# Batch 3's tails are cast and turned earlier, batch 5's loads move to GpSimd's queue (sliding-window attention, then a GELU block)

## Chip, cores and metric

The kernel runs on one core of a Trainium2 chip. The metric is device time in microseconds, as the median of several runs; a profile of one further execution comes with it. Engines are named as in the profile: PE is TensorE (PEld its weight loads), DVE is VectorE, ACT is ScalarE, POOL is GpSimd and SP is SyncE, whose queue of DMA issues is SPq.

## The reference

```python
# q, k, v: (8 batches, 8 heads, 576 positions, 64), fp32
scores = (q @ k.T) / 8                        # per batch and head
mask = |pos_i - pos_j| <= 32                  # others get -1e9
attn = softmax(scores);  x = attn @ v         # -> x: (4608 tokens, 512)
h = x @ w_in                                  # (512, 2048)
g = 0.5 * h * (1 + tanh(sqrt(2/pi) * (h + 0.044715 * h**3)))
out = g @ w_out                               # (2048, 512), fp32
```

## The kernel before

The 4608 tokens are nine tiles of 512. Tile `t` of the second part (`w_in`, Gelu, `w_out`) runs while the attention of batch `b = t + 1` is worked on between its matmuls, so a batch is always one tile ahead. The order of all instructions on every engine is written out by hand (the pools run in manual schedule); waits between engines follow from the tiles that instructions read and write.

A tile has two stretches. In the first, `ffn_in` makes 16 blocks of 128 hidden columns, four matmuls of 128x512 each (L594), and ScalarE takes the Gelu of each (L602). Its loop over `fc` carries extra steps of the attention at given `fc`. In tiles 3 and up this stretch is written as a list of steps (`MIX_1`, run by `in_mixed`), in which step `keys` of tile 3 turns batch 4's keys and issues batch 5's loads, and step `tails` turns batch 4's tails. In the second stretch, a loop over `i` from 0 to 111 issues one matmul of the product with `w_out` each (L794; seven products of 16 matmuls instead of eight), and a plan (`PLAN_1` for tile 1, `PLAN_2` for tile 2, `PLAN` after) says at which `i` a score (`s`), a mask (`m`), a weighing (`v`) or a spread (`x`) of the next batch comes. Scores `s0` and `s1` stand at `i == 7`, `s2` at 35, `s3` and the score of the tails, `s4`, at 63; `b0` and `b1`, casts of the next batch's keys, at 63 too.

The attention needs queries and keys transposed. Positions 0 to 511 and the last 64 (the tails) go separate ways:

- Batches 1 to 3 have their tails of queries and keys in one tile `tr`. `cast_tails` (L358) casts it to fp16 as `t`, `trans_tails` transposes it on TensorE (L363), and ScalarE copies the result to `KL` and `QT` (L365, L367).
- From batch 4 on, tails are cast by VectorE (L419 for queries, L446 for keys) and transposed by DMA on SyncE's queue: `turn_queries` (L422) writes `QT`, `turn_key_tails` (L447) writes `KL`.
- The other positions are cast by VectorE (`turn_query` L427, `turn_keys` L437) and transposed by DMA on SyncE's queue (L431 to `QT`, L439 to `KT`, two pairs of heads at a time).

`load_qk(b)` issues the loads of a batch's queries (L208, 1 MB in one transfer) and keys (L200, four transfers of 256 KB); `load_tails` those of the tails (L214, L215 from batch 4 on). SyncE's queue works in the order of the program. GpSimd's queue carries the loads of the values, cast to fp16 on the way (`load_v` L223, `load_vt` L227), and the stores of the output (`store`, L754 and L756). Ahead of each batch's `load_v` GpSimd copies one column of `KL` to a tile `after` (L1039), which makes the load wait for that `KL`. In tile 1 GpSimd also casts batch 3's values (L1043).

The output tile `y` is stored in eight transfers a tile: four for the part C21 when it is done (L826, at `i == 95`), four at the tile's end in `ffn_last` (after L835).

Of the kernel before, what the change touches and what calls it, by code (L numbers as in the profile page):

```python
# [84 lines left out]
def kernel(  # L85
# [9 lines left out]
    nc = tc.nc  # L95
# [87 lines left out]

        return qk, tails, vs

    def load_qk(b):


        if b == 3:
            qr = raws[3]  # L190
        else:
            qr = rawp.tile([128, H, 256], FP32, name="qr", tag="q0")
            load_q(b, qr)
        kr = rawp.tile([128, 4, H, 64], FP32, name="kr", tag="k1" if b == 3 else "k0")
        if b > 3:
            raws[b] = [qr, kr]
        else:
            raws[b] = [qr, kr, tailp.tile([128, H, 64], FP32, name="tr", tag="tr"), None]
        for c in range(4):
            nc.sync.dma_start(kr[:, c, :, :],  # L200
                              k[b, :, 128 * c:128 * c + 128, :].rearrange("h p d -> p h d"))
        if b < 5:
            load_tails(b, nc.sync)
        if b == 3:
            load_vr(3)

    def load_q(b, qr):
        nc.sync.dma_start(qr, q[b, :, 0:512, :].rearrange("h (p j) d -> p h (j d)", j=4))  # L208

    def load_tails(b, queue):  # L210
        if b > 3:
            raws[b] += [tailp.tile([16, H, 256], FP32, name="qt", tag="vt"),
                        tailp.tile([64, H, 64], FP32, name="kt", tag="tr")]
            queue.dma_start(raws[b][2], q[b, :, 512:576, :].rearrange("h (p j) d -> p h (j d)", j=4))  # L214
            queue.dma_start(raws[b][3], k[b, :, 512:576, :].rearrange("h p d -> p h d"))  # L215
        else:
            queue.dma_start(raws[b][2][0:64, :, :], q[b, :, 512:576, :].rearrange("h s d -> s h d"))
            queue.dma_start(raws[b][2][64:128, :, :], k[b, :, 512:576, :].rearrange("h s d -> s h d"))
# [136 lines left out]
    def cast_tails(b, copy, half=slice(0, 128)):  # L355
        if len(halfs[b]) < 3:
            halfs[b].append(hp.tile([128, H, 64], FP16, name="t16", tag="t16"))
        copy(halfs[b][2][half, :, :], raws[b][2][half, :, :])  # L358
# [50 lines left out]
    def load_vr(b):  # L409
        vr = vrs[b] = rawp.tile([128, 4, H, 64], FP32, name="vr", tag="q1")  # L410
        for c in range(4):
            nc.sync.dma_start(vr[:, c, :, :],
                              v[b, :, 128 * c:128 * c + 128, :].rearrange("h p d -> p h d"))
# [36 lines left out]
    def open_and_turn(b):  # L450
        cast_open(b)
        for pr in range(NPAIR):
            turn_query(b, pr)
# [117 lines left out]
    def column(t, n):  # L571

        return n // 2 + 8 * (n % 2) if t else n
# [79 lines left out]
    def in_mixed(t):  # L653
        if "B" not in mixed:
            mixed["B"] = rawp.tile([128, 3, 512], FP32, name="sb", tag="q1")
        if t == NT - 2:
            mixed["A"] = rawp.tile([128, 3, 512], FP32, name="sa", tag="k0")

        place = {"00": (0, "b"), "01": (1, "c"), "11": (2, "c")}
        for step in MIX if t >= NT - 2 else MIX_1:  # L660
            kind, rest = step[0], step[1:]
            if step == "pair":
                pair_v(t + 1, nc.vector.tensor_copy)
            elif step == "load":
                if 3 < t < B - 2:
                    load_qk(t + 2)
            elif step == "keys":
                if t == 3:
                    turn_keys(4)
                    load_qk(5)  # L670
            elif step == ("f0" if t > 3 else "tails"):
                turn_queries(t + 1)
                if t == 3:
                    turn_key_tails(4)
                    load_tails(5, nc.sync)
            elif step == "f1":
                if t > 3:
                    turn_key_tails(t + 1)
                    if t + 2 < B:
                        load_tails(t + 2, nc.sync)  # L680
            elif step in ("f0", "tails"):
                pass
            elif kind in UNITS:
                in_product(kind, int(rest), t < NT - 2)
            elif kind == "s":
                n, unit = int(rest[0]), rest[1]
                (nc.scalar.copy if n == 1 or rest == "3B" else nc.vector.tensor_copy)(
                    mixed[unit][:, (0, 1, None, 2)[n], :], phs[unit, "a"])
            elif kind == "c":
                x, which = place[rest[1:]]  # L690
                x = mixed[rest[0]][:, x, :]
                nc.vector.tensor_tensor(x, phs[rest[0], which], x, op=ALU.add)
            elif kind == "g" and rest[0] in UNITS:
                r, c, j = int(rest[1]), int(rest[2]), UNITS[rest[0]]
                src = phs[rest[0], "a"] if rest[1:] == "10" else mixed[rest[0]][:, place[rest[1:]][0], :]
                nc.scalar.activation(gTs[t][:, 8 * r + 2 * j:8 * r + 2 * j + 2, 256 * c:256 * c + 256],
                                     src.rearrange("p (h c) -> p h c", h=2), AF.Gelu_apprx_tanh)
            elif kind == "g":
                fc = column(t, int(rest))
                nc.scalar.activation(gTs[t][:, fc, :], phs[fc], AF.Gelu_apprx_tanh)  # L700
            elif kind in PARTS:
                sums(t, int(rest), PARTS[kind])
            else:
                ffn_in(t, int(step), then=False)
# [271 lines left out]
    for t in range(NT):  # L976
        b = t + 1
        att = b < B
        if t:
            for fc in range(begun):  # L980
                ffn_in(t, fc, 3, 4, then=False)
            for fc in range(begun):
                gelu(t, fc)
            if b == 2:
                open_and_turn(2)
                combine(2, nc.vector)
                combine(3, nc.vector)
            elif att:
                if t >= LONE:
                    in_x(t)  # L990
                if b == 3:
                    turn_keys(b)
            if t >= NT - 2:
                if t == NT - 2:
                    in_x(t)
                in_mixed(t)
            elif t >= LONE:
                in_mixed(t)
            for fc in range(begun, NF if t < LONE else 0):
                ffn_in(t, fc)  # L1000
                if t == 1 and fc == 3:
                    turn_keys(2)
                    load_vr(2)
                    raws[2] = [None, None, raws[2][2], vrs[2], tailp.tile([64, H, 64], FP32, name="vt", tag="vt")]
                    nc.sync.dma_start(raws[2][4], v[2, :, 512:S, :].rearrange("h p d -> p h d"))
                    raws[3] = rawp.tile([128, H, 256], FP32, name="qr", tag="q0")
                    load_q(3, raws[3])
                    combine(4, nc.vector)
                if t == 1 and 6 <= fc < 10:
                    cast_v(2, fc - 6)  # L1010
                if t == 1 and fc == 6:
                    trans_tails(1, psO.tile([128, 8, 128], FP16, name="pt", tag="O"))
                if t == 1 and fc == 8:
                    cast_tails(2, nc.scalar.copy)
                if t == 1 and fc == 13:
                    trans_tails(2, psO.tile([128, 8, 128], FP16, name="pt", tag="O"), copy=nc.scalar.copy,
                                copy_q=nc.scalar.copy)
                if t == 2 and fc == 8:
                    cast_tails(3, nc.gpsimd.tensor_copy)
                if t == 2 and fc == 13:  # L1020
                    trans_tails(3, psO.tile([128, 8, 128], FP16, name="pt", tag="O"), copy=nc.scalar.copy,
                                copy_q=nc.scalar.copy)
                if t == 2 and fc == 8:
                    pair_v(b, nc.vector.tensor_copy)
                if t == LONE - 1 and fc in (8, 9, 10, 11):
                    in_w(nc.vector, "B", (8, 9, 10, 11).index(fc) + 1)
# [7 lines left out]
        if t in (1, 2):  # L1034
            load_qk(b + 1)
        ods = {}
        for i in range(113 if t else 65):
# [5 lines left out]
                    nc.gpsimd.tensor_copy(Vs[1][:, c, :, :], vrs[3][:, c, :, :])  # L1043
            if t == 1 and i == 98:
                open_and_turn(3)
            for act in plan.get(i, "").split():
                kind, at = act[0], int(act[act.index("@") + 1:]) if "@" in act else None
                g = int(act[1:].split("@")[0])
# [52 lines left out]
                elif kind == "v":  # L1101
                    bb, gg = group(g)
                    o, d = weigh(bb, gg, at)
# [59 lines left out]
```

## Time and profile before

| | |
|---|---|
| median of 3 runs | 296.35 us (295.05 to 297.62) |
| profiled execution | 296.1 us, span 294.2 us |
| TensorE's granted clock, mean | 0.992 |
| tile 2's Gelu stretch | about 86 to 100 us |
| tile 3's Gelu stretch, then its `w_out` stretch | about 117 to 131 us, 131 to 148 us |

A stretch's times are read from the windows of the profile. In a timeline, a line gives start and duration in us, the engine, the line of the kernel, the operation, output and inputs, and how many instructions of a kind were merged; square brackets hold the idle time of the engine before it and what ended it. For the queue of SyncE a line's duration is the time that the issue took, not the transfer; a transfer lands later.

### The profile page before, as it was taken

To read this page: it belongs to the slowest core of one execution; us is meant where nothing else is said; L and a number is where in the kernel's file an instruction comes from. 1 tells how busy PE (TensorE), PEld (TensorE's weight loads), DVE (VectorE), ACT (ScalarE), POOL (GpSimd) and SP (SyncE) were. 2 spreads that over 40 slices of the span, in tenths; PEclk is the share of its full clock that TensorE was granted. 3 is DMA by queue.
4 is the path that set the end of the run, shared out by engine and by line. 5 is a ranking of instruction groups with operands and counts; after the bars stand their busy time and mean duration, and the time that the engine had idled before them with its cause. 6 is when DMAs were issued, how large, how long until landed. Compare 5 with 4: busy or idle time off the path is not lost.

```text
span 294.2 us, 7438 instructions
## 1 busy us (share of the span) xinstructions
PE 285.1 (97%) x2993; PEld 197.4 (67%) x2993; DVE 227.5 (77%) x499; ACT 197.0 (67%) x323; POOL 87.7 (30%) x143
## 2 busy tenths in 40 slices
PE   8889999999999999999999999999999999999993
PEld 3535544557875588668766886688667877887783
DVE  4565369898987977998878798889888877875672
ACT  4875767879477776587558955895579667905800
POOL 3434325102228821400662236015600060016000
PEclk9979999999999999999999999999999999999998
DMA  7999998999999999999999799999930022005013
GB/s 217 265 332 411 353 305 223 254 183 197 253 224 190 234 223 184 215 216 168 140 176 269 163 144 208 234 124 115 192 83 2 3 73 72 0 3 144 0 47 98
DMA packets 114392, 51.02 MB, mean 173 GB/s; under 512 B 98471, under 2 KB 110247, under 8 KB 114102
## 3 DMA queue, kind: packets, MB, share of 16 engines
q1 hardware_dynamic: 89460, 38.67, 58.9%
q0 software_dynamic: 23776, 10.83, 23.3%
q10 hardware_dynamic: 1122, 1.06, 1.1%
q8 instruction: 23, 0.38, 0.6%
q14 instruction: 11, 0.09, 0.1%
HBM read 36.70 MB, written 9.44 MB: 157 GB/s over the span
## 4 chain that ended last, share of the span: by engine, by line
PE 81%; DMA 7%; SPq 5%; POOL 3%; issue 1%; DVE 1%; ACT 0%; ACTq 0%; POOLq 0%
PE mm L794 28%; PE ph L594 16%; PE mm L594 13%; PE pu L650 7%; DMA vr<-in_v_dram 4%; PE ps_s L485 3%; PE py L766 3%; PE mm L766 2%; SPq L200 2%; PE ps_d L512 2%; PE ps_o L522 2%; DMA qr<-in_q_dram 2%; DMA KL<-kt 2%; PE mm L650 1%; POOL out_dram L756 1%; PE ps_od L512 1%
## 5 line engine op out<-in xcount | busy, mean ns | idle before, releaser
L594 PEld LDWEIGHTS <-w_in 128*128 128x128 f16 x448 | 50.2, 113 | 38.7
L594 PE MATMUL ph<-xT,w_in 128*128 128x512 f16 x240 | 60.2, 379 | 0.0
L594 PE MATMUL mm<-xT,w_in 128*128 128x512 f16 x208 | 53.7, 379 | 0.0
L794 PEld LDWEIGHTS <-s 128*128 128x128 f16 x512 | 49.4, 98 | 6.1
L756 POOL DMA_DIRECT2D out_dram<-y x55 | 30.4, 561 | 72.1 <-DVE y L826 63.0
L794 PE MATMUL mm<-t,s 128*128 128x256 f16 x376 | 44.9, 273 | 0.0
L794 PEld LDWEIGHTS <-gT 128*128 128x128 f16 x384 | 36.1, 98 | 6.6 <-issue 0.2
L498 ACT ACTIVATE pe<-ps_s 128x960 f16<-128x960 f32 (+1 forms) x31 | 29.6, 976 | 14.0 <-PE ps_s L485 13.8
L602 ACT ACTIVATE gT<-mm 128x512 f16<-128x512 f32 x28 | 16.5, 599 | 24.8 <-PE mm L594 24.5
L794 PE MATMUL mm<-w_out,gT 128*128 128x256 f16 x256 | 32.6, 273 | 0.0
L737 DVE TENSOR_TENSOR s<-gT 128x512 f16<-128x512 f16 x64 | 27.3, 432 | 6.4 <-ACT gT L602 3.0
L602 ACT ACTIVATE gT<-ph 128x512 f16<-128x512 f32 x38 | 20.9, 606 | 7.0 <-PE ph L594 7.0
L110 ACT ACT_TABLE_LOAD x18 | 23.1, 1283 | 2.2 <-issue 1.9
L547 ACT ACTIVATE lt<-ps_d 128x480 f32<-128x480 f32 (+2 forms) x28 | 15.5, 555 | 12.6 <-PE ps_d L512 7.7
L548 ACT ACTIVATE lt<-lt 128x480 f32<-128x480 f32 (+3 forms) x36 | 21.1, 586 | 1.1
L507 DVE TENSOR_TENSOR pe<-pe,band 128x960 f16<-128x960 f16 x28 | 17.7, 651 | 2.7 <-ACT pe L498 2.6
L522 PEld LDWEIGHTS <-V 128*64 128x64 f16 x520 | 14.2, 113 | 6.2 <-DVE V L233 1.6
L700 ACT ACTIVATE gT<-ph 128x512 f16<-128x512 f32 x22 | 13.2, 601 | 4.8 <-PE ph L594 4.7
L794 PE MATMUL mm<-t,gT 128*128 128x256 f16 x128 | 16.2, 273 | 0.0
L557 DVE TENSOR_TENSOR xT<-ps_o,lt 128x480 f16<-128x480 f32 (+5 forms) x26 | 13.4, 533 | 3.2 <-PE ps_o L522 2.8
L1039 POOL COPY after<-KL 128x1 f16<-128x1 f16 x4 | 1.2, 312 | 45.8 <-DMA KL<-kt 44.9
L223 POOL DMA_DIRECT2D V<-in_v_dram x16 | 14.3, 909 | 1.1 <-PE ps_o L522 0.4
(154 smaller groups left out, 488.5 us busy)
## 6 DMA issues: line engine op xcount, KB each, us to landing
kr<-in_k_dram SPq DMA_DIRECT2D x31, 256.0 KB, 6.3
qr<-in_q_dram SPq DMA_DIRECT2D x6, 1024.0 KB, 8.2
wst<-in_moe_w_in_dram SPq DMA_DIRECT2D x8, 512.0 KB, 6.6
vr<-in_v_dram SPq DMA_DIRECT2D x12, 256.0 KB, 6.0
wst<-in_moe_w_out_dram SPq DMA_DIRECT2D x2, 1024.0 KB, 11.6
wst<-in_moe_w_out_dram SPq DMA_DIRECT2D x4, 512.0 KB, 7.2
V<-in_v_dram POOLq DMA_DIRECT2D x16, 128.0 KB, 5.2
qr<-in_q_dram SPq DMA_DIRECT2D x7, 256.0 KB, 8.2
```

Of the source, the lines that this page charges most:

```text
L110: nc.scalar.add_instruction(mybir.InstLoadActFuncSet(name=nc.get_next_instruction_name(), act_func_set_id=which, ins=[], outs=[]))
L498: nc.scalar.activation(pe, ps[:, :, 0:w], AF.Exp, scale=SCALE)
L507: nc.vector.tensor_tensor(pe, pe, m.rearrange("k (o j) p -> k o j p", o=1).broadcast_to(list(pe.shape)), op=ALU.mult)
L522: nc.tensor.matmul(o[64 * h:64 * h + 64, cols].rearrange("d (j p) -> d j p", j=4)[:, :, p0 - q0:p1 - q0], Vs[b % 2][:, slot, 2 * pr + h, : ...
L547: nc.scalar.activation(lt[:, 0:n], d[:, 0:n], AF.Ln)
L548: nc.scalar.activation(lt[:, 0:n], lt[:, 0:n], AF.Exp, scale=-1.0)
L594: nc.tensor.matmul(ph, w_cols[:, dc, fc // 4, fc % 4, :], xT[:, dc, t * 512 % RING:t * 512 % RING + 512], start=(dc == 0), stop=(dc == 3))
L602: nc.scalar.activation(gTs[t][:, fc, :], phs[fc], AF.Gelu_apprx_tanh)
L650: nc.tensor.matmul(ps[:, 256 * h:256 * h + 256], lhs[:, d, h, :], rhs[:, d, :], start=(n in (0, 2, 4) and h == d == 0), stop=(h == d == 1) ...
L737: nc.vector.tensor_tensor(dst, x, y, op=op)
L756: eng.dma_start(out_v[b, j, q0 + p:q0 + p + e, cols], yo[m:m + e, cols])
L794: nc.tensor.matmul(pys["apart"][:, 0:256] if apart else py[:, blk, :], lhsT, wino[w][:, f, :], start=(new and i % (8 if one else 16) == 0) ...
```

## The change

Two moves. The cast of batch 3's tails (`cast_tails(3)`, on GpSimd in both versions) goes from block 8 of tile 2 to `i == 98` of tile 1, in the program's order behind the stores of C21 and ahead of the four of `ffn_last`; their transposes on TensorE, with ScalarE's two copies, go from behind block 13 of tile 2 to behind block 10. And `load_qk` takes a queue: batch 5's queries and keys, five transfers, are issued by GpSimd in place of SyncE, at the same step `keys` of tile 3. Its tails stay on SyncE's queue.

```diff
-    def load_qk(b):
+    def load_qk(b, queue=nc.sync):
...
-            load_q(b, qr)
+            load_q(b, qr, queue)
...
-            nc.sync.dma_start(kr[:, c, :, :],
+            queue.dma_start(kr[:, c, :, :],
...
-    def load_q(b, qr):
-        nc.sync.dma_start(qr, q[b, :, 0:512, :].rearrange("h (p j) d -> p h (j d)", j=4))
+    def load_q(b, qr, queue=nc.sync):
+        queue.dma_start(qr, q[b, :, 0:512, :].rearrange("h (p j) d -> p h (j d)", j=4))
...
                 if t == 3:
                     turn_keys(4)
-                    load_qk(5)
+                    load_qk(5, nc.gpsimd)
...
-                if t == 2 and fc == 8:
-                    cast_tails(3, nc.gpsimd.tensor_copy)
-                if t == 2 and fc == 13:
+                if t == 2 and fc == 10:
                     trans_tails(3, psO.tile([128, 8, 128], FP16, name="pt", tag="O"), copy=nc.scalar.copy,
                                 copy_q=nc.scalar.copy)
...
             if t == 1 and i == 98:
                 open_and_turn(3)
+                cast_tails(3, nc.gpsimd.tensor_copy)
```

## The prediction

> **What bounds the kernel now.** I read the page's first part, then the chain of work that ended last, then the list of waits of TensorE in the part of the span that the change touches, and then the timelines of the engines that it moves work between. The page says that TensorE is the wall:
>
> ```profile
> PE 285.1 (97%) x2993; PEld 197.4 (67%) x2993; DVE 227.5 (77%) x499; ACT 197.0 (67%) x323; POOL 87.7 (30%) x143
> ...
> PE 81%; DMA 7%; SPq 5%; POOL 3%; issue 1%; DVE 1%; ACT 0%; ACTq 0%; POOLq 0%
> ```
>
> No other engine is near 97%, so a gain can only come out of TensorE's idle time. The waits of TensorE from 86 us to the end of the span (who waited for whom, us in total, times, longest) are two:
>
> ```profile
> PE ps_s L485 <- DMA KL<-kt: 0.7, 1, 0.7
> PE pt L363 <- POOL t L358: 0.4, 1, 0.4
> ```
>
> The timelines show both. First the tails of batch 3 in tile 2 (start, duration, and in brackets the idle time before):
>
> ```profile
> 92.89 2.14 POOL L756 DMA_DIRECT2D out_dram<-y  x4
> 95.01 0.76 POOL L754 DMA_DIRECT2D out_dram<-y  x1
> 95.77 1.66 POOL L756 DMA_DIRECT2D out_dram<-y  x3
> 97.43 0.85 POOL L358 CAST t<-tr 128x512 f16<-128x512 f32 x1
> ...
> 98.33 0.40 PE L363 MATMUL pt<-idn,t 128*128 128x128 f16 x4 [0.45 <-POOL t L358]
> ```
>
> GpSimd issues tile 1's eight stores, then casts; TensorE waits 0.45 us for the cast. Second, the keys' tail of batch 4 in tile 3, as SyncE's queue and TensorE show it:
>
> ```profile
> 127.36 0.57 SPq L208 DMA_DIRECT2D qr<-in_q_dram  x1
> 128.03 6.30 SPq L200 DMA_DIRECT2D kr<-in_k_dram  x4
> 134.43 1.92 SPq L422 DMA_TRANSPOSE QT<-qt  x1
> 136.44 2.25 SPq L447 DMA_TRANSPOSE KL<-kt  x1
> ...
> 140.99 0.23 PE L485 MATMUL ps_s<-QT,KL 64*64 64x96 f16 x2 [0.72 <-DMA KL<-kt]
> ```
>
> The transpose that writes KL is issued behind batch 5's five loads and lands at 140.95; TensorE stood ready at 140.27. After that TensorE has no wait left to the end, so what is taken away at these two places reaches the end whole, and 0.45 + 0.72 = 1.17 us is all that there is to win.
>
> **The change, part by part.** *Cast and turn of batch 3's tails.* The moved instruction is one cast (0.85 us). In the changed program's order GpSimd runs it after the four C21 stores (92.89 to 95.01) and ahead of the other four, not ahead of all eight. Those four cannot be earlier either: the chain of work leads into them from L1043's casts, which wait for batch 3's values, landed at 90.53. So the cast runs at about 95.01 to 95.86, 2.42 us earlier than now. But TensorE asks for it earlier too. Without its stall it reaches the transposes at 98.33 - 0.45 = 97.88; a block of four matmuls is 0.865 us (96.86 to 94.27 is three blocks), so behind block 10 it reaches them at 97.88 - 2.59 = 95.29. The cast's end and the 0.05 us that TensorE needs after it give 95.91, so it waits 0.62 us in place of 0.45: **0.17 us lost**. Bounds: the chain shows 0.34 us of "issue" before 95.01, so a cast might start at 94.67; GpSimd's casts of this case took 0.60 (L347, 64 partitions) to 0.96 us (L1043). That gives a wait of 0.03 to 0.77 us, or -0.42 to +0.32. I take the row of the same cast, 0.85. Its cover: the two ScalarE copies behind the transposes (0.37 and 0.38 us) come between Gelus that wait 0.27 us for TensorE, thus three Gelus absorb them as now. The four stores that the cast passes go out 0.85 us later, about 104.95 instead of 104.10 for the last landing; VectorE writes their buffer again at 105.68 (L807), so 0.7 us of cover remains. The values' loads (L223) start 0.9 us earlier, since GpSimd ends with a store at 98.28 and the copy "after" no longer waits for ScalarE's KL; they land before batch 4's last keys (119.09) in either case. Both at nothing.
>
> *Batch 5's loads on GpSimd's queue.* SyncE loses five issues (127.36 to 134.33). Its next step, L422, waits for VectorE's four L419 casts, which end at 130.35, so it goes out near 130.4 instead of 134.43, four microseconds earlier; with the same 1.92 and 2.25 us of issue, L447 ends near 134.7 and lands, with the 2.26 us that it took here from the end of its issue, at 137.0. TensorE wants it at 140.27 (+0.17): a margin of 3.4 us, **0.72 us won**. Bounds: 0 to 0.72. GpSimd gains five issues. The nearest row is its own values' load with as many rows:
>
> ```profile
> 141.62 3.57 POOL L223 DMA_DIRECT2D V<-in_v_dram  x4
> ```
>
> 0.89 us each, 4.5 us in all, in a stretch in which it is idle (121.25 to 141.07). They wait there for earlier transfers of the same lane (lanes are used in turn, eight of them): the first for the store of 116.32, which landed at 120.64, the fourth and fifth for stores that landed at 124.58 and 127.11. So the queries' load goes out near 121.3 and the last keys near 127.2 to 128.1, where SyncE's last was out at 134.33. Behind them on GpSimd stand only the copy "after", which waits for KL (earlier now), the values' loads and the stores of 147: nothing is late by that. The total of bytes is the same.
>
> What the trace does not show is fp32 loads from GpSimd's queue beside SyncE's transposes. These share the 16 DMA engines. Batch 4's transposes for the queries and keys are issued at 117.60, 121.62 and 126.04 and land at 128.19, 128.50 and 129.71, with the stores of GpSimd's queue beside them until 128.2. The stores stand ahead of the new loads in that queue, so little changes before 127. The nearest row with loads in GpSimd's queue is batch 5's keys: issued at 144.57 and 146.33 beside the V loads they landed 8.0 and 10.6 us later. With these the first keys would land at 129.6 (needed at 131.2) and the second at 136.7 (needed by s2 at 135.4, late by 1.3 us). Best case 129.71 as now, worst 136.7: cost 0 to 1.3 us. I take 0, since the loads stand behind the stores and batch 4's transposes are mostly done when they begin; batch 5's met the V loads from their start.
>
> The loads must land for VectorE's key casts at 141.01 (now 139.34 for the last). From 128.1 as the last issue with the L200's longest landing of 12.8 us it would be 140.9: just in time. VectorE could be held until 142.8 before its mask L507 (142.77, read by TensorE at 145.22, 0.65 us long) is late, so I cost it at nothing.
>
> The Trainium skill, "SBUF — State Buffer", section on the two separate sides, under "A bandwidth-pool intuition that's wrong (but worth ruling out)", says that GpSimd cannot write a transfer's descriptors while VectorE holds their shared port, and gives about 3.1 us for a transfer that takes 0.62 alone. The 0.89 us above was measured beside VectorE's casts L427 and L437, so the trace does not show that here. By the page's figure the five would take 15.5 us, an estimate, and end near 137.
>
> **Sum.** +0.17 - 0.72 = -0.55 us. The profiled execution took 296.1 us with a span of 294.2, so it would take 295.55. The median of the runs is 296.35, 0.25 above the profiled one; on that scale the forecast is 295.8 us.
>
> **Rivals.** *The tails' wait goes as well* (cast starts at 94.67 and is short): -0.42 - 0.72 = -1.14, 295.2 us. For it, the 0.34 us of "issue"; against it, 0.85 for this very cast.
>
> *KL is as late as now*: its transpose shares the engines with loads that are still moving. For it, L422 in tile 4 needed 6.6 us from issue to landing with GpSimd's stores beside it; against it, 3.4 us of margin. Then +0.17, 296.5 us.
>
> *Slower: batch 4's keys are turned late because GpSimd's loads mix with the transposes.* Place: score s2 at 135.4 us, and before it s0 at 131.2. It decides from a landing later than 135.4 + 0.55. By batch 5's row it is 1.3 us; with KL then in time anyway, 1.3 + 0.17 - 0.72 = +0.75, 297.1 us; if the first pair is late by as much again as its margin (1.6 us), it is +2.4, 298.7. For it, batch 5's 8.0 and 10.6 us, and the 4.3 us that the first key transpose needed only to be issued here; against it, the stores ahead of the loads in the queue.
>
> *GpSimd's issues are held up by a busy VectorE*: if each took 3.6 us, what now four take together, the five would end near 139.3 and the last keys land 6.3 us later (L200's median), at 145.6; VectorE, in order, would hold its mask 2.8 us past the slack of 142.8: +2.25 us, 298.6. Against it, 0.89 us beside a busy VectorE. This is the rule of the Trainium skill's SBUF page above; the trace so far speaks against it.
>
> **How the numbers follow.** Forecast 0.47; tails' wait gone 0.10; KL as late as now 0.17; keys turned late 0.18; issues held up 0.08. All but the dear ends of the last two lie within 1% (2.96 us, about what a measurement of this kernel can tell from no change, its three runs spreading from 295.05 to 297.62). A gain over 1% would need more than all of TensorE's waits here: 0.03, for noise. Slower by over 1%: half of the last two, 0.13. Within: 0.84. The range goes from 294.8 (the best case less 0.4 for noise) to 298.4, just short of the dear ends; the forecast's own is 294.9 to 296.7.
>
> **What would show it.** Right: TensorE's wait before L363 about 0.6 us, behind block 10; GpSimd's cast between its fourth and fifth store; L422 issued near 130.4 and KL landed before 138; no wait of TensorE for KL, KT or QT in tile 3; span near 293.65. Wrong: a wait of TensorE at s0 or s2 of tile 3 on a KT transpose; the new loads taking over 1.5 us each on GpSimd; VectorE waiting at L437 for kr; or a wait before L363 under 0.2 us.

## The result and the profile after

The changed kernel takes 305.72 us (median of 6 runs, 304.97 to 308.07) against 296.06 us for the kernel before on the same chip; the ratio is 1.0353 (95% interval 1.0298 to 1.0408). In this document a ratio leaves out runs more than 1.5% above the fastest of their kernel, a median has them in. The profiled execution took 305.65 us with a span of 303.8 us, 9.6 us more than before. The page's first part and chain of the kernel after, to be read beside those of before:

```profile
PE 285.3 (94%) x2993; PEld 198.1 (65%) x2993; DVE 227.2 (75%) x499; ACT 196.8 (65%) x323; POOL 91.7 (30%) x148
...
PE 69%; DMA 14%; SPq 6%; DVE 5%; POOL 2%; issue 2%; ACT 1%; ACTq 0%; DVEq 0%; POOLq 0%
```

TensorE does the same work (285.3 us) but now has idle time, and transfers stand for twice the share of the chain. The waits of TensorE from 80 us on are these two (us in total, times, longest):

```profile
PE ps_s L485 <- DMA KT<-k: 9.6, 1, 9.6
PE mm L794 <- DVE y L817: 0.2, 1, 0.2
```

Neither of the two waits of before is left: not the one at L363 and not the one for KL. In their place stands one of 9.6 us for KT, the keys of batch 4, at the first scores of tile 3, which the prediction had named as a sign that it is wrong. The chain of the kernel after around that place (start, duration):

```profile
119.48 0.86 PE mm L594 x4
120.34 0.15 PE pu L650 x2
120.49 19.02 DMA KT<-k
139.51 0.04 issue
139.55 1.01 PE ps_s L485 x24
```

The transpose that writes KT's first pair is issued at 120.49 us and lands 19.02 us later; in the kernel before it took 6.9 us (121.62 to 128.50). The timelines of GpSimd and of SyncE's queue in the kernel after show what stands beside it:

```profile
120.19 0.93 POOL L208 DMA_DIRECT2D qr<-in_q_dram  x1 [0.33 <-DMA out_dram<-y]
121.12 1.78 POOL L200 DMA_DIRECT2D kr<-in_k_dram  x2
124.93 1.76 POOL L200 DMA_DIRECT2D kr<-in_k_dram  x2 [2.03 <-DMA out_dram<-y]
...
116.07 4.32 SPq L431 DMA_TRANSPOSE QT<-q  x1
120.49 10.23 SPq L439 DMA_TRANSPOSE KT<-k  x2
130.81 2.24 SPq L422 DMA_TRANSPOSE QT<-qt  x1
133.14 1.19 SPq L447 DMA_TRANSPOSE KL<-kt  x1
```

GpSimd issues the five loads without trouble, 0.9 us each. SyncE's two key transposes need 10.23 us to be issued, 5.69 before. L422 goes out at 130.81, right behind them, and lands only at 142.40; KL lands at 143.01. The transposes of the tails are thus late too, as those of the keys are.

The wait costs more than its length. In the windows of the kernel after (us, busy us of each engine with its count, then TensorE's granted clock, DMA share and GB/s) the clock falls while TensorE stands:

```profile
130.00:134.00 4.00, 0.00 (x0) 0.00 (x0) 2.20 (x7) 1.08 (x1) 0.00 (x0) 1.00 1.29 133
134.00:144.30 10.30, 4.75 (x57) 3.51 (x58) 0.88 (x2) 2.74 (x4) 0.84 (x2) 0.50 1.15 92
144.30:148.00 3.70, 3.70 (x71) 2.99 (x70) 2.71 (x5) 1.64 (x3) 3.57 (x5) 1.00 1.22 79
```

TensorE stops at 129.91 and goes on at 139.55, so for about 4.7 us after the wait the clock is at a half. From s0 to the score of the tails TensorE needs 150.60 - 139.55 = 11.05 us; before it was 140.99 - 131.22 - 0.72 of waiting = 9.05. So 2.0 us are lost to the clock. "TensorE: Matmul & The Clock Gate" of the Trainium skill, under "What's actually happening", says that the clock halves after an idle stretch of some 3.4 us and comes back after as much work. Here it halved about 4.1 us after TensorE stopped and came back 4.7 us after it went on; but in run e1 below a wait of 2.45 us, which ended at 96.18, was already followed by 3.4 us at half:

```profile
97.30:100.70 3.40, 3.40 (x10) 1.19 (x9) 2.12 (x5) 1.19 (x2) 3.40 (x7) 0.50 0.99 223
```

The books: + 9.64 (wait) + 2.0 (clock) + 0.2 (L817) - 0.72 (KL) - 0.45 (L363) = + 10.7. The span grew by 9.6. Of the difference 1.1 us are no work of the change: block 10 of tile 2 begins at 93.15 us in this execution and at 94.27 in that of before, ahead of any changed instruction of TensorE or GpSimd.

### The profile page after: what moved, and what is told of

Same layout as the page of the kernel before. It is cut to its first block, busy times and chain, and to the rows that moved or that the text cites. A ratio compares the mean times of both kernels' runs of the same rounds, so it can differ in the third digit from the quotient of the medians.

```text
span 303.8 us, 7446 instructions
## 1 busy us (share of the span) xinstructions
PE 285.3 (94%) x2993; PEld 198.1 (65%) x2993; DVE 227.2 (75%) x499; ACT 196.8 (65%) x323; POOL 91.7 (30%) x148
## 4 chain that ended last, share of the span: by engine, by line
PE 69%; DMA 14%; SPq 6%; DVE 5%; POOL 2%; issue 2%; ACT 1%; ACTq 0%; DVEq 0%; POOLq 0%
PE mm L794 27%; PE ph L594 12%; PE mm L594 9%; DMA KT<-k 6%; PE pu L650 6%; DMA vr<-in_v_dram 4%; PE ps_s L485 3%; PE mm L766 2%; DMA wst<-in_moe_w_in_dram 2%; PE py L766 2%; SPq L200 2%; PE ps_d L512 2%; SPq L278 2%; DVE t L727 1%; DMA qr<-in_q_dram 1%
## 5 line engine op out<-in xcount | busy, mean ns | idle before, releaser
L794 PE MATMUL mm<-w_out,gT 128*128 128x256 f16 x256 | 33.6, 278 | 0.0
L737 DVE TENSOR_TENSOR s<-gT 128x512 f16<-128x512 f16 x64 | 26.5, 419 | 6.6 <-ACT gT L602 3.2
L485 PE MATMUL ps_s<-QT,KT 64*64 64x128 f16 (+3 forms) x576 | 13.9, 220 | 9.9 <-DMA KT<-k 9.6
L485 PEld LDWEIGHTS <-KT 64*64 64x64 f16 x576 | 10.3, 109 | 15.8 <-DMA KT<-k 9.9
L737 DVE TENSOR_TENSOR s<-s,gT 128x512 f16<-128x512 f16 x32 | 14.3, 446 | 1.1
```

The source lines that it names most:

```text
L485: nc.tensor.matmul(sides[h][64 * half:64 * half + 64, 4 * n * r:4 * n * r + 4 * n].rearrange("k (j p) -> k j p", j=4)[:, :, p0 - q0:p1 - q ...
L737: nc.vector.tensor_tensor(dst, x, y, op=op)
L794: nc.tensor.matmul(pys["apart"][:, 0:256] if apart else py[:, blk, :], lhsT, wino[w][:, f, :], start=(new and i % (8 if one else 16) == 0) ...
```

## Experiments

Theory A: the DMA engines serve GpSimd's and SyncE's queues packet by packet in turn; GpSimd's fp32 loads travel as packets of 4096 bytes, a DMA transpose as packets of 256, so the transposes get hardly any of the bytes until the loads are through. Theory B: any second queue with 2 MB would do as much. Each run has one profile, so a wait given below is that of a single execution.

**e1: the tails' half alone.** Edit: the changes of `cast_tails(3)` and `trans_tails(3)`, with batch 5's loads left as before.

> The change's first half alone: batch 3's tails cast and turned earlier, batch 5's loads left on SyncE's queue. Theory A and theory B (below, on the loads) both lay the whole loss on the loads, so no wait of TensorE for KT in tile 3, the 0.72 us for KL as before, and a wait before L363 between 0 and 0.6 us instead of 0.45: 295.6 to 296.5 us. A theory C, in which the earlier turn moves the values' loads forward and so helps to spoil batch 4's transposes, would show a wait for KT here too: over 298 us.

296.68 us, a little over the range, ratio 1.0005 (0.9966 to 1.0044). So this half is worth nothing that can be measured, and the loss is not from it. Its profile has no wait for KT, and shows why the gain can't be relied on; the wait before L363 was 2.45 us, beyond the range expected:

```profile
91.45 0.61 POOL L1041 CAST V<-vr 128x512 f16<-128x512 f32 x1 [0.49 <-DMA vr<-in_v_dram]
92.01 2.60 POOL L756 DMA_DIRECT2D out_dram<-y  x4
94.60 1.52 POOL L358 CAST t<-tr 128x512 f16<-128x512 f32 x1
...
96.18 0.40 PE L363 MATMUL pt<-idn,t 128*128 128x128 f16 x4 [2.45 <-POOL t L358]
```

The cast stands behind four stores that stand behind casts that wait for batch 3's values, and here it took 1.52 us, beside copies and sums of VectorE. Where it comes relative to TensorE changes from run to run: no wait in the kernel after, 2.45 us here.

**e2: the loads' half alone.** Edit: `load_qk(5, nc.gpsimd)`, tails as before.

> The change's second half alone: batch 5's five loads on GpSimd's queue, the tails as before. Theory A (the loads travel in GpSimd's queue as packets of 4096 bytes, the DMA transposes of batch 4's keys as packets of 256 bytes, the DMA engines take packets from the two queues in turn, so the transposes get a small share) and theory B (any 2 MB that move beside the transposes hold them up, in whatever packets) agree: a wait of TensorE for KT<-k of 9 to 10 us, 305 to 306.5 us. Theory C (both halves are needed for the loss) expects under 299 us.

306.77 us, ratio 1.0349 (1.0281 to 1.0417), a wait for KT of 8.7 us; both lie 0.3 us outside the ranges. The whole loss is in this half. Its packets from 124 to 135 us by queue (packets, MB, share of 16 engines; q0 is GpSimd's queue, q1 SyncE's):

```profile
q0 software_dynamic: 699, 2.23, 89.8%
q1 hardware_dynamic: 533, 0.13, 8.2%
```

Over this window the two queues are near one packet each (699 to 533), and GpSimd's moves 17 times the bytes. But this is an average of two unlike stretches, 124 to 130 us and 130 to 135 us:

```profile
q0 software_dynamic: 353, 1.04, 87.9%
q1 hardware_dynamic: 103, 0.02, 3.3%
...
q0 software_dynamic: 346, 1.20, 92.1%
q1 hardware_dynamic: 430, 0.11, 14.1%
```

First GpSimd's queue has 3.4 packets for one, then SyncE's has a few more. In the kernel after, from 123 to 135 us, they are 653 to 1184. So the rows show that the transposes get a small share while these loads move, but not that the queues take strict turns. In the kernel before, with SyncE's queue alone from 127 to 130 us, it moved 1820 packets in 3 us:

```profile
q1 hardware_dynamic: 1820, 0.62, 109.8%
```

And from 141 to 153 us of the kernel before, the stretch in which batch 5's keys are transposed beside the casting loads of V:

```profile
q0 software_dynamic: 4714, 0.66, 82.2%
q1 hardware_dynamic: 4312, 1.08, 66.0%
```

Again near one each over the window, but there GpSimd's packets are 128 bytes, and it moves 0.66 MB. "DMA: Bandwidth & Descriptors" of the Trainium skill, under "Queues, rings and completion order", states that an engine changes between queues at whole packets; the uneven counts above neither show that nor rule it out.

**e3: the loads on ScalarE's queue.** Edit: `load_qk(5, nc.scalar)`, at the step `load`; the first load went out at 123.56 us, against 122.31 in e2.

> Batch 5's five loads on ScalarE's queue, the tails as before: a second queue beside SyncE's again, but one whose fp32 loads travel as packets of 1024 (queries) and 256 bytes (keys), as SyncE's do. They are issued at the step load, about 3 us behind the step keys, so that ScalarE's Gelus do not wait for VectorE's casts. Theory A: the transposes get about half of the packets, KT's first pair lands by 131.5 and TensorE waits under 1.5 us for it; ScalarE's issues may cost 1 to 3 us by themselves, seen as waits of TensorE for ScalarE. Theory B: the wait for KT<-k is over 5 us, as with GpSimd's queue.

309.8 us, ratio 1.0432 (1.0361 to 1.0504). The issues cost far more than the 1 to 3 us expected, and the loss has this reason of its own, in the timelines of ScalarE and TensorE:

```profile
124.05 9.80 ACTq L201 DMA_DIRECT2D kr<-in_k_dram  x4
133.90 1.08 ACT L702 ACTIVATE gT<-mm 128x512 f16<-128x512 f32 x2 [9.83 <-DMA kr<-in_k_dram]
...
134.55 1.86 PE L595 MATMUL mm<-xT,w_in 128*128 128x512 f16 x4 [8.55 <-ACT gT L702]
```

ScalarE was held 9.8 us by issuing four loads, and TensorE waited for its Gelus. KT's first pair landed at 132.82 (A: by 131.5), 9.9 us after its issue at 122.93 and not 18.6 as in e2 (122.42 to 141.03). In that time GpSimd's and ScalarE's queues moved 1.86 MB, in e2 GpSimd's 2.67. From 128 to 134 us ScalarE's queue (q10) and SyncE's had the same number of packets:

```profile
q10 hardware_dynamic: 2065, 0.89, 73.5%
q1 hardware_dynamic: 2074, 0.52, 53.8%
```

That speaks for A. But TensorE came to the scores only after this hold, so whether a wait for KT would have stayed under 1.5 us is not shown.

**e4: GpSimd's queue, small packets.** Edit: `qr` and `kr` of batch 5 are fp16 tiles, so the loads cast on the way and travel as packets of 512 and 128 bytes.

> Batch 5's loads on GpSimd's queue at the same place, the tails as before, but into fp16 tiles: the transfer casts, as it does for the values. The rows read from DRAM are the same, the packets are then 128 bytes (keys) and 512 bytes (queries) instead of 4096. VectorE's casts of these tiles become copies. Theory A: the transposes keep their turns; KT's first pair lands near 129.6 to 132 and TensorE waits under 1.5 us; 295.5 to 298 us. Theory B: a wait for KT<-k over 5 us, over 301 us.

300.85 us, ratio 1.0152 (1.0077 to 1.0227), with a wait for KT of 3.1 us in the fastest of its four runs (298.93 to 303.37), where A expected under 1.5 and B over 5. So the same rows on the same queue at the same place cost 3.1 us in place of 8.7. But casting loads also write half as many bytes, so this run alone can't say whether the smaller packets or the fewer bytes cut the wait. The counts show how far A goes. From 128 to 133 us, the queries' 512 bytes, and from 133 to 135, the keys' 128 bytes:

```profile
q0 software_dynamic: 1171, 0.52, 130.0%
q1 hardware_dynamic: 499, 0.12, 37.1%
...
q0 software_dynamic: 836, 0.11, 82.1%
q1 hardware_dynamic: 779, 0.21, 79.0%
```

With 128 bytes the queues are even (836 to 779), with 512 bytes GpSimd's has 2.3 packets for one. One each in turn, as A has it, does not hold for that size; why is open.

**e5 and e6: the queries alone, the keys alone.** Edit: one of the two on GpSimd's queue, the other on SyncE's as before.

> Only batch 5's queries (1 MB, one transfer) on GpSimd's queue, its keys on SyncE's queue behind the transposes of batch 4's keys as before; tails as before. Theory A (the two queues are served in turn, and a turn of GpSimd's fp32 loads is 4096 bytes against 256 of a transpose): 256 packets of 4096 bytes, half of the change's 512, so about half of the loss: a wait for KT<-k of 2 to 5 us, 297.5 to 301 us. Theory D (the keys' rows of 256 bytes are what makes GpSimd's queue costly: its packets took 250 to 1150 ns each late in the changed kernel, against 180 for the queries'): a wait under 1.5 us, under 297.5 us.

> Only batch 5's keys (four transfers, 1 MB) on GpSimd's queue, its queries on SyncE's queue as before; tails as before. Theory A: 256 packets of 4096 bytes, about half of the loss, a wait for KT<-k of 2 to 5 us, 297.5 to 301 us. Theory D: nearly all of the loss, a wait of 7 us or more, over 303 us.

e5: 299.06 us (nine runs, 295.94 to 305.36), ratio 1.0083 (1.0038 to 1.0128), wait for KT 2.6 us. e6: 298.58 us, ratio 1.0109 (1.0053 to 1.0164), wait 2.6 us. That the keys' rows are at fault is refuted. The two halves add up to less than the whole (5.2 us of 8.7), and the landings say why. TensorE asks at 130.7 us in e5 and at 132.3 in e6, and has some slack: in the kernel before KT landed 2.7 us ahead of it. The table has KT's first pair, from its issue to its landing, with the bytes that GpSimd's and ScalarE's queues moved in that time, stores included:

| run | new loads: queue, packets in bytes | KT landed | us from issue | MB beside it | last new load landed |
|---|---|---|---|---|---|
| before | none | 128.50 | 6.9 | 0.58 | |
| e3 | 2 MB, ScalarE, 1024 and 256 | 132.82 | 9.9 | 1.86 | 137.97 |
| e6 | 1 MB, GpSimd, 4096 | 134.86 | 11.7 | 1.62 | 136.31 |
| e5 | 1 MB, GpSimd, 4096 | 133.22 | 12.1 | 1.62 | 132.41 |
| e4 | 1 MB written, GpSimd, 512 and 128 | 133.34 | 13.0 | 1.14 | 143.07 |
| e2 | 2 MB, GpSimd, 4096 | 141.03 | 18.6 | 2.67 | 140.85 |
| after | 2 MB, GpSimd, 4096 | 139.51 | 19.0 | 2.66 | 141.22 |

Beside loads of 4096-byte packets KT lands within 1.7 us of the last of them. The first megabyte adds about 5 us, of which the slack covers 2.7; the second adds about 7, paid nearly in full. Neither theory orders all rows. Bytes alone do not: e3 has more than e5 and e6 beside KT and is earlier, e4 has fewer and is later. Packet size alone does not either: e4's are the smallest. e4 shares GpSimd's queue with e2, e5 and e6, and e3 does not, so a cause in that queue itself is a rival that no run here tests.

**e7: the loads behind the transposes.** Edit: `nc.gpsimd.tensor_copy(after, KTs[0][:, 3, 0:1])` ahead of the loads.

> All five loads on GpSimd's queue as in the change, tails as before, but ahead of them GpSimd copies one column of KT's last pair, so that they are issued only when the transposes of batch 4's keys have landed (about 129.8 us). Theory A: the waits for KT are gone, since nothing moves beside these transposes; the loads then run beside the two transposes of the tails, which are issued from 130.4 on, so KL lands later than in the kernel before and TensorE waits 1 to 3.5 us for it: 296.5 to 299.5 us. If instead the wait for KT stays over 5 us, the cause is not the overlap in time but something else in the order of the queues, and theory A falls.

301.55 us, over the range expected, ratio 1.0183 (1.0122 to 1.0244). The wait for KT is gone (first pair landed at 131.06, second at 131.91), as A has it: with the same loads on the same queue, only the overlap in time is missing, so this overlap is the cause. The price came at another place than expected, in the timelines of VectorE and TensorE:

```profile
147.35 0.76 DVE L438 CAST k<-kr 128x512 f16<-128x512 f32 x2 [4.08 <-DMA kr<-in_k_dram]
...
148.76 2.93 PE L796 MATMUL mm<-t,gT 128*128 128x256 f16 x13 [3.39 <-DVE y L819]
```

The last keys landed at 147.06, VectorE waited 4.08 us for them in its order, and TensorE 3.39 us for the sum behind them. KL landed at 141.27 and held nobody.

**e8: the same aim on one queue.** Edit: SyncE's order is queries' load, the tails' two transposes, then the keys' four loads; VectorE's casts b0 and b1 stand at step 80 of tile 3.

```diff
-        for c in range(4):
-            nc.sync.dma_start(kr[:, c, :, :],
-                              k[b, :, 128 * c:128 * c + 128, :].rearrange("h p d -> p h d"))
+        if b != 5:
+            load_k(b, kr)
...
                     turn_key_tails(4)
+                    load_k(5, raws[5][1])
                     load_tails(5, nc.sync)
```

`load_k` holds the four loads that stood in `load_qk`.

> What the change aimed at, without GpSimd's queue: everything on SyncE's, the queries' load where it was, the two transposes of batch 4's tails behind it, and the four loads of batch 5's keys behind those; VectorE's first casts of these keys (b0, b1) come at step 80 instead of 63 of tile 3, as they land later. Tails of batch 3 as before. Within one queue the transposes stand ahead of the loads and share with nothing but stores: KL lands near 137, no wait of TensorE for KL or KT, so 0.7 us less than before: 294.9 to 296.3 us, which the runs may not tell from no change; the profile does.

295.77 us, ratio 0.9987 (0.9957 to 1.0017). KL landed at 134.55, and no wait for KL or KT is in the profile. The profile has two other waits of TensorE, 1.0 us in all, for the sum that stands at L817 before; they come at 173.5 and 204.1 us, in later tiles than the edit, and what caused them is not shown. The span is as before (294.3 to 294.2).

**e9 and e10: the cast ahead of the values' casts.** Edit, alone (e10) and with that of e8 (e9): `cast_open(3)` and `cast_tails(3)` at `i == 94` ahead of L1043, the transposes behind block 13 as before.

> The run with keys loaded behind the tails' transposes on SyncE's queue, and with the cast of batch 3's tails put on GpSimd ahead of its casts of batch 3's values (it waits only for loads that landed by 87 us), turned behind block 13 as before. Both waits of TensorE that the change aimed at should be gone, L363 <- POOL (0.45 us or more) and KL (0.72 us): 1.2 us less than before, 294.0 to 295.6 us, with a ratio of 0.993 to 0.999. A rival: VectorE's copies of V and the values' casts on GpSimd come 0.85 us later behind the cast, and the wait turns up elsewhere: 295.5 to 296.5 us.

> The kernel before with one edit: the cast of batch 3's tails on GpSimd ahead of its casts of batch 3's values, turned behind block 13 as before, batch 5's loads on SyncE's queue as before. No wait of TensorE before L363, the wait for KL as before: 0.5 us less than before, 295.2 to 296.2 us, which the runs may not tell from no change.

e10: 296.89 us, ratio 1.0001 (0.9963 to 1.0039). e9: 295.47 us, ratio 0.9936 (0.9894 to 0.9978), ahead of the kernel before and of the change. TensorE's waits in e9 from 80 us on:

```profile
PE pu L656 <- DVE sb L694: 1.2, 1, 1.2
PE mm L801 <- DVE y L824: 0.2, 1, 0.2
```

The waits for L358, KL and KT are gone, and 1.2 us of another, for VectorE, has come. It stands at 122.40 us in tile 3, and VectorE's timeline shows what it goes back to:

```profile
120.32 1.43 DVE L443 CAST k<-kr 128x512 f16<-128x512 f32 x4 [1.23 <-DMA kr<-in_k_dram]
121.67 0.68 DVE L694 COPY sb<-pu 128x512 f32<-128x512 f32 x1
```

VectorE waits for the load of batch 4's keys, and TensorE for VectorE. In e10 VectorE waits 0.70 us at the same place and TensorE 0.7. The last of these keys landed at 120.20 us in e9 and at 120.85 in e10, against 119.09 before; whether the edit made them late is not shown. So what is won at the tails is lost again some 25 us later, at the next transfer. TensorE's wait for KL, which e10 was expected to have as before, did not appear in its profile, though the order of the loads is unchanged. The spans are 293.7 (e9), 294.2 (e10) and 294.2 us (before). That e9 came out ahead rests on its ratio alone; the medians of all runs are 295.47 and 296.73, and its profiled execution had a granted clock of 1.0 against 0.992 of before. A gain is thus not shown.

## Why the prediction was wrong

- *What bounds the kernel* was right: TensorE, with two waits to be won. Both vanished in the kernel after.
- *The tails*: the sum gave a wait of 0.62 us as if it were fixed. Profiles showed 0 and 2.45 for the same code; the cast stands behind casts that wait for loads, and their landing differed (GpSimd's last cast of values ended at 91.4 and 92.1 us). Its effect on the time can't be told from nothing (e1).
- *The issues*: five at 0.9 us, as forecast; GpSimd was not held up by VectorE, and that rival is out. The 3.1 us that the Trainium skill gives in "SBUF — State Buffer" ("A bandwidth-pool intuition that's wrong") were not seen in any run here; the longest issue on GpSimd took 1.25 us (e4). The prediction's own evidence was misread, though: the four V loads were issued from 141.62 on, and VectorE's casts L427 had ended at 141.09, L437's first two at 141.76, so most of the 0.89 us stood beside sums and masks.
- *L422 near 130.4* came true (130.81) by luck. The forecast had it wait for VectorE's casts, which ended at 128.97 in the kernel after; what held it was SyncE's issue of the KT transposes, until 130.72. In e2 the same hold let it out only at 135.48.
- *KL won by 0.72 us*: it landed at 143.01, not at 137.0. It cost nothing only because TensorE was later still.
- *The term that failed is "I take 0"* for transposes beside the new loads, with its upper bound of 1.3 us; TensorE waited 9.64 us at s0. The reason given was that batch 4's transposes are mostly done when the loads begin. The prediction's own times speak against it: the queries' load near 121.3, the first key transpose at 121.62. In the kernel after they were issued at 120.19 and 120.49, so the key transposes went out with the loads and not ahead of them (e7 shows that without this overlap the wait is gone).
- *The bound* came from batch 5's keys beside the V loads as the nearest row. That row has the right queue and the right number of rows, but 0.66 MB in packets of 128 bytes, because V is cast on the way; the new loads are 2 MB in packets of 4096. The rival "keys turned late" named the mechanism and the place, s0 and s2 of tile 3; its price of 1.3 to 2.9 us of lateness started from the same row.
- *"The stores stand ahead of the new loads, so little changes before 127"* was wrong as well. The stores had packets of 4096 bytes too, and the transposes of before were already slow beside them: SyncE's queue moved 459 packets from 124 to 127 us and 1820 from 127 to 130, when no store was left. The prediction had the 4.3 us that the first key transpose needed to be issued and used it for the rival alone.
- *Left out altogether*: the clock. No term of the sum held the stretch at half clock behind a long wait (2.0 us).

## What to carry to other kernels

Moving a transfer to another queue does not only take it out of the way of what stood behind it; it lets it move beside what stood ahead of it. Before that, look in the rows for what will be under way at the same time, and ask which of the two transfers has a consumer waiting; here a DMA transpose beside 2 MB of GpSimd's loads took 19 us in place of 7. Take as nearest row one with as many bytes and the same packets, not only the same queue. Changing the order inside one queue brought no such wait (e8, e9), though no gain of it over the kernel before is shown. A long new wait of TensorE costs its length and a stretch at half clock.

## What the runs showed of the hardware

- The same fp32 load travels as packets of 1024 (queries) or 256 bytes (keys) when SyncE or ScalarE issues it, and as 4096 when GpSimd does; with a cast to fp16, GpSimd's are 512 and 128.
- The more of GpSimd's 4096-byte loads moved beside a DMA transpose, the later it landed: 6.9 us after its issue with none, 11.7 and 12.1 with 1 MB, 18.6 and 19.0 with 2 MB. Packet counts of two queues were near even in some stretches (836 to 779 in e4, 2065 to 2074 in e3) and not in others (353 to 103 in e2, 1171 to 499 in e4), so turns of one packet each are not shown as a rule.
- An engine can be held long by issuing transfers: ScalarE 9.8 us for four loads (e3), SyncE 10.23 us for two transposes (after). What held them is not shown.
- A wait of TensorE of 2.45 us (e1) was followed by 3.4 us at half clock; one of 9.64 us (after) by 4.7 us, the clock having halved 4.1 us into the wait.
